# Attention pieces between matmuls: scores, the next pair's q and k, a pause, values in one piece, a pause, probabilities eight at a time

## The chip, the cores and the metric

The kernel runs on one core of a Trainium2 chip. The metric is the device time of one execution in microseconds, as the median of several runs. The kernel before takes 888.13 us (three runs, 887.55 to 888.17).

## What is computed

Three stages follow each other: an attention over 4 batches of 8 heads (576 tokens, 64 elements a head), a feed-forward layer with a gated activation, and a second, bilinear feed-forward layer. The attention is the sum of two: one over means of 4 neighbouring tokens, repeated 4 times, and one over the 7 tokens that lie closer than 4.

```python
q_d = q.reshape(B, H, Sd, factor, D).mean(axis=3)        # the same for k and v; factor = 4
out_up = np.repeat(sm_attn(q_d, k_d, v_d), factor, axis=2)
mask = np.abs(pos[:, None] - pos[None, :]) < factor
scores = np.where(mask, scale * np.matmul(q, k.transpose(0, 1, 3, 2)), -1e9)
attn_out = out_up + np.matmul(softmax(scores), v)

h = x @ w_in;  x = (h * sigmoid(1.702 * h)) @ w_out      # 2304 tokens, 512 -> 2048 -> 512
x = ((x @ w1) * (x @ w2) @ w3) @ w_out2                  # 512 -> 1024 -> 1024 -> 512
```

## The kernel before

Two heads form a pair, so there are 16 pairs, four to a batch. Tokens go through the feed-forward layers in five blocks of 512, 512, 512, 256 and 512. All large products are made of three matmuls of 128 rows (high times low, low times high, high times high; mm3, L118 to L120), with weights that are decoded and split by ACT, DVE and POOL. The weights come from float64 words: DVE decodes them with L173, L176 and L179, which write st and dec. Three staging buffers st and two dec take turns once the first 24 weights are through.

The order of the large work is: the product w34 = w3 times w_out2 (16 steps, each transposed on TensorE from a decoded w3 tile, copied by ACT at L574 and completed by DVE at L575, names w3t and ps_w); then blocks 0 to 4 of the first feed-forward layer (h_step and y_step, names ps_h, ps_y, g_t, gl); then the second layer (ps_ab, ps_o). "Block 0" is always the first token block.

The attention is cut into pieces, and a pump puts one piece after every three matmuls (in the w34 product, which carries batch 0) or after every six (blocks 0 to 2, which carry batches 1 to 3). An entry None in the list is a pause: nothing is put there. A pair goes through four stages:
- T: q and k are transposed into qT and kT, in four pieces (two for q, two for k). In batches 0 and 1 TensorE does it (L284, ps_t) and ACT copies the result (L285); in batches 2 and 3 DVE does it (L280). The means qd and kd are summed on POOL (L294, L296) or on DVE.
- S: three pieces. Two of local scores (L333, ps_s; DVE masks them at L336 into el and takes the maximum at L337) and one of pooled scores (L352, ps_sp). Then the softmax: with own_exp ACT makes one exponential for each of 15 tiles and sums as it goes (L313, after three L311 on DVE); without own_exp DVE subtracts the maximum (L358 for ep, L362 for el), ACT makes two large exponentials (L364, L366) and DVE sums them (L367, L369). L371 and L372 form the reciprocal; POOL (DVE in batch 3) multiplies el and ep with it (L375, L377).
- P: the probabilities are transposed on TensorE (L395, ps_pt) in pieces of up to four tiles and copied by ACT into PT (L396). The first piece also sums the means of v on POOL (v_means).
- V: three pieces. Pooled values (L410, ps_vp, ACT copies od at L413) and two of local values (L422, ps_v; DVE adds od into xo at L426; a DMA writes it to x_d, from where the blocks read it).

The tiles ps_t, ps_s, ps_sp, ps_pt, ps_vp and ps_v all come from one pool of two PSUM buffers, tag t. xo and the results w34s of the w34 product share two buffers, tag ys. The pairs 12 to 15 (batch 3) have no local scores on TensorE; DVE and POOL compute these in small steps beside the blocks.

The stages are lined up in att_pieces: S of a pair, V of the pair before, T of the next pair, P of the pair. The loads of q and k are issued in p_piece and s_pool, two pairs ahead. own_exp is set for batch 0, not for batch 1, and for batches 2 and 3.

The instructions are put in order, engine by engine, when the program is built, by a scheduler that works from the code's order and from priorities; what stands in a queue is therefore shown from the order of the built program.

## Time and profile before

| | us |
|---|---|
| median of 3 runs | 888.13 |
| the profiled execution | 892.31 |
| its span, first to last instruction | 890.5 |
| TensorE (PE) busy | 846.0 (95%) |
| DVE busy | 589.5 (66%) |
| ACT busy | 408.7 (46%) |
| POOL busy | 150.6 (17%) |

A share over the whole span says little here: from about 470 us on TensorE works without a gap, and all of the attention lies before that. The rows below are therefore taken by stretches: 0 to 56 us (first weights, a third of the w34 product), 56 to 120 us (the rest of it, batch 0), 120 to 262 us (block 0, batch 1). Block 1 with batch 2 ends near 381 us. Busy times of matmuls are modelled and overlap; distances from start to start are firmer.

### The profile page before, as it was taken

How to read it: one execution, taken by the hardware profiler on the slowest of the kernel's cores; microseconds unless marked ns; L12 is line 12 of the kernel's file. 1: busy time of each engine (PE TensorE's matmuls, PEld its weight loads, DVE VectorE, ACT ScalarE, POOL GpSimd, SP SyncE). 2: the span in 40 equal slices, each digit the busy share in tenths (PEclk: the TensorE clock that was granted, in tenths of full speed). 3: DMA queues.
4: the chain of work that ended last, by engine and by line, in shares of the span. 5: the costliest groups of instructions: out<-in, count | busy, mean ns of one | idle time of the engine just before them, and what ended most of it. 6: DMA issues, size and time to landing. Idle time of an engine off the chain costs nothing.

```text
span 890.5 us, 13711 instructions
## 1 busy us (share of the span) xinstructions
PE 846.0 (95%) x5132; PEld 712.1 (80%) x5132; DVE 589.5 (66%) x1053; ACT 408.7 (46%) x862; POOL 150.6 (17%) x153
## 2 busy tenths in 40 slices
PE   5789979999999999999999999999999999999998
PEld 4567757666677777777789988889999899989996
DVE  5997587889998795847758973253456455555551
ACT  4667567567657665455446663342112211232111
POOL 7524241244332323311200000000000000000000
PEclk9799999999999999999999999999999999999999
DMA  8865584565656243553348989102556364635521
GB/s 239 270 207 160 155 249 129 163 182 170 158 156 123 63 108 87 131 126 62 78 148 304 358 325 348 49 1 86 210 196 259 105 244 166 255 135 222 191 84 71
DMA packets 140598, 150.76 MB, mean 169 GB/s; under 512 B 86898, under 2 KB 121460, under 8 KB 136436
## 3 DMA queue, kind: packets, MB, share of 16 engines
q1 hardware_dynamic: 119424, 141.21, 49.1%
q10 hardware_dynamic: 21108, 8.69, 4.0%
q8 instruction: 40, 0.66, 0.3%
q14 instruction: 26, 0.21, 0.1%
HBM read 117.75 MB, written 32.11 MB: 168 GB/s over the span
## 4 chain that ended last, share of the span: by engine, by line
PE 72%; DVE 12%; DMA 7%; issue 3%; ACT 3%; POOL 2%; ACTq 0%; SPq 0%; DVEq 0%; POOLq 0%
PE ps_ab L120 7%; PE ps_ab L118 7%; PE ps_ab L119 7%; PE ps_h L118 6%; PE ps_y L118 5%; PE ps_y L120 5%; PE ps_h L119 5%; PE ps_y L119 5%; PE ps_h L120 5%; PE ps_o L120 4%; PE ps_o L119 4%; PE ps_o L118 4%; DMA st<-in_moe_w_in_dram 3%; DVE dec L179 2%; DVE st L176 2%
## 5 line engine op out<-in xcount | busy, mean ns | idle before, releaser
L118 PE MATMUL ps_h<-x_t,w 128*128 128x512 f32 (+1 forms) x320 | 122.7, 385 | 3.0 <-DVE w L115 2.0
L118 PE MATMUL ps_y<-gh,w 128*128 128x512 f32 (+1 forms) x320 | 122.5, 383 | 0.0
L119 PE MATMUL ps_h<-x_t,w 128*128 128x512 f32 (+1 forms) x320 | 119.2, 372 | 1.1 <-DVE x_t L115 1.1
L119 PE MATMUL ps_y<-gl,w 128*128 128x512 f32 (+1 forms) x320 | 118.8, 371 | 0.4 <-DVE gl L115 0.4
L120 PE MATMUL ps_y<-gh,w 128*128 128x512 f32 (+1 forms) x320 | 119.2, 372 | 0.0
L120 PE MATMUL ps_h<-x_t,w 128*128 128x512 f32 (+1 forms) x320 | 118.5, 370 | 0.0
L120 PE MATMUL ps_ab<-b_t,a_in 128*128 128x384 f32 x336 | 112.5, 335 | 0.0
L118 PE MATMUL ps_ab<-b_t,a_in 128*128 128x384 f32 x336 | 112.5, 335 | 0.0
L119 PE MATMUL ps_ab<-b_t,a_in 128*128 128x384 f32 x336 | 112.4, 334 | 0.0
L115 DVE TENSOR_TENSOR gl<-g_t,gh 128x512 fp32r<-128x512 f32 (+1 forms) x80 | 55.0, 690 | 65.8 <-ACT gh L114 65.5
L624 ACT ACTIVATE g_t<-ps_h 128x512 f32<-128x512 f32 (+1 forms) x80 | 44.3, 555 | 92.0 <-PE ps_h L120 87.9
L114 ACT ACTIVATE abh<-ab 128x384 fp32r<-128x384 f32 x24 | 12.7, 527 | 137.5 <-DVE ab L749 137.5
L118 PEld LDWEIGHTS ps_h<-x_t,w 128*128 128x128 f32 x320 | 60.5, 190 | 17.2 <-DVE w L115 3.7
L118 PEld LDWEIGHTS ps_y<-gh,w 128*128 128x128 f32 x320 | 60.5, 189 | 11.8 <-issue 2.4
L119 PEld LDWEIGHTS ps_h<-x_t,w 128*128 128x128 f32 x320 | 60.8, 190 | 11.0 <-DVE x_t L115 2.2
L120 PEld LDWEIGHTS ps_y<-gh,w 128*128 128x128 f32 x320 | 60.5, 189 | 10.4
L120 PEld LDWEIGHTS ps_h<-x_t,w 128*128 128x128 f32 x320 | 60.5, 189 | 10.4 <-issue 0.2
L119 PEld LDWEIGHTS ps_y<-gl,w 128*128 128x128 f32 x320 | 60.6, 189 | 9.3 <-DVE gl L115 0.5
L118 PEld LDWEIGHTS ps_ab<-b_t,a_in 128*128 128x128 f32 x336 | 63.1, 188 | 0.9
L119 PEld LDWEIGHTS ps_ab<-b_t,a_in 128*128 128x128 f32 x336 | 63.1, 188 | 0.9
L179 DVE SCALAR_TENSOR_TENSOR dec<-dec,st 128x512 int32<-128x512 int32 x72 | 59.3, 833 | 6.0 <-ACT dec L166 4.8
L120 PEld LDWEIGHTS ps_ab<-b_t,a_in 128*128 128x128 f32 x336 | 63.1, 188 | 0.0
(150 smaller groups left out, 1667.3 us busy)
## 6 DMA issues: line engine op xcount, KB each, us to landing
a_in<-a_d SPq DMA_DIRECT2D x24, 1792.0 KB
st<-in_moe_w_dram SPq DMA_DIRECT2D x32, 512.0 KB
a_d<-ap SPq DMA_DIRECT2D x8, 1792.0 KB
st<-in_moe_w_out_dram SPq DMA_DIRECT2D x24, 512.0 KB
st<-in_moe_w_in_dram SPq DMA_DIRECT2D x16, 512.0 KB
yr<-y_d SPq DMA_DIRECT2D x12, 384.0 KB
out_dram<-osb SPq DMA_DIRECT2D x17, 256.0 KB
s_v<-in_v_dram ACTq DMA_DIRECT2D x15, 288.0 KB
```

Source lines behind the costliest of these rows:

```text
L114: nc.scalar.activation(hi, raw, AF.Copy)
L115: lo_eng.tensor_tensor(lo, raw, f32(hi), op=ALU.subtract)
L118: nc.tensor.matmul(ps, ll, rh, start=start, stop=False, skip_group_check=more)
L119: nc.tensor.matmul(ps, lh, rl, start=False, stop=False, skip_group_check=more)
L120: nc.tensor.matmul(ps, lh, rh, start=False, stop=stop, skip_group_check=more)
L176: nc.vector.scalar_tensor_tensor(low, st[:, :, 1], -0x80000000, low, op0=ALU.bitwise_and, op1=ALU.bitwise_or)
L179: nc.vector.scalar_tensor_tensor(t, t, 3, st[:, :, 0], op0=ALU.logical_shift_left, op1=ALU.bitwise_or)
L624: nc.scalar.activation(g[:, :n], ps[:, :n], AF.Gelu_apprx_sigmoid)
```

## The change

- The order in att_pieces becomes: S of a pair, T of the next pair, two pauses, V of the pair before, three pauses (two in batch 0), P of the pair.
- T has two pieces instead of four: both halves of q at once, then both halves of k. Each is followed by the load of the next pair's q or k, which leaves p_piece and s_pool.
- V is one piece, v_all: pooled and local values go into two PSUM buffers without a break, the pooled ones and the second local half in one buffer; then od, then the two xo, second half first. For the pairs of batch 3, v_far does the pooled values as before.
- P is done up to eight tiles at a time, with a pause between.
- Batch 0 no longer uses own_exp.

```diff
@@ t_piece, s_pool, p_piece: the loads of q and k
+            if 0 < n < B * HP - 1:
+                att_load(n + 1, name)
...
-        if n % HP == 0 and n > 0:
-            att_load(n + 1, "qk")
...
-            if n % HP < HP - 1 and n + 2 < B * HP:
-                att_load(n + 2, "qk")
@@ values
+    def v_all(n):
+
+        both = pst.tile([128, NB], F32, tag="t", name="ps_v")
+        rest = pst.tile([128, NB], F32, tag="t", name="ps_v")
+        local = ((HQ, NQB, both[:, SD:SD + (NQB - HQ) * QB]), (0, HQ, rest[:, :HQ * QB]))
+        v_pool_mm(n, both[:, :SD])
+        for i0, i1, ps in local:
+            v_local_mm(n, i0, i1, ps)
+        v_pool(n, both[:, :SD])
+        for i0, i1, ps in local:
+            v_local(n, i0, i1, ps)
+        if n + 1 < B * HP and n + 1 not in LOCAL:
+            att_load_v(n + 1)
@@ stage
+        def together(*fns):
+            return [None] * (len(fns) - 1) + [lambda: [fn() for fn in fns]]
+
         if what == "T":
-            return [lambda name=name, c=c: t_piece(n, name, c) for name in "qk" for c in range(2)]
+            return [together(*(
+                lambda name=name, c=c: t_piece(n, name, c) for c in range(2)))[-1] for name in "qk"]
...
         if what == "P":
-            return [lambda i=i: p_piece(n, i, min(i + 4, NPT)) for i in range(0, NPT, 4)]
-        return [lambda: v_pool(n), lambda: v_local(n, 0, HQ), lambda: v_local(n, HQ, NQB)]
+            return [p for i in range(0, NPT, NPH) for p in together(*(
+                lambda i=i: p_piece(n, i, min(i + 4, NPT)) for i in range(i, min(i + NPH, NPT), 4)))][1:]
+        return [lambda: v_all(n)]
@@ att_pieces
             out_ += stage(n0 + i, "S", own_exp)
+            if i + 1 < HP:
+                out_ += stage(n0 + i + 1, "T", own_exp)
+            out_ += [None] * 2
             if i > 0:
                 out_ += stage(n0 + i - 1, "V", own_exp)
-            if i + 1 < HP:
-                out_ += stage(n0 + i + 1, "T", own_exp)
-            else:
-                out_ += [None] * rest
+            out_ += [None] * (2 if b == 0 else 3)
             out_ += stage(n0 + i, "P", own_exp)
@@ batch 0
-        pump = Pump(att_pieces(0, True, 3))
+        pump = Pump(att_pieces(0, False, 3))
```

Three places show what this does to the order. The first is TensorE at the start of block 0, where pair 4, the first of batch 1, begins: s_k is its k, ps_t the transpose, ps_s and ps_sp its local and pooled scores. Before:

```order
L120 MATMUL ps_h<-x_t,w 128x512
L284 MATMUL ps_t<-ident,s_k 128x72 x4
L118 MATMUL ps_h<-x_t,w 128x512
L119 MATMUL ps_h<-x_t,w 128x512
L120 MATMUL ps_h<-x_t,w 128x512
L284 MATMUL ps_t<-ident,s_k 128x72 x4
L333 MATMUL ps_s<-kT,qT 64x72 x18
L352 MATMUL ps_sp<-kd,qd 64x144 x6
L118 MATMUL ps_h<-x_t,w 128x512 x2
```

After, from the second local piece on (the transposes of s_k stand 24 full matmuls ahead of it):

```order
L335 MATMUL ps_s<-kT,qT 64x72 x8
L118 MATMUL ps_y<-gh,w 128x512
L119 MATMUL ps_y<-gl,w 128x512
L120 MATMUL ps_y<-gh,w 128x512
L118 MATMUL ps_y<-gh,w 128x512
L119 MATMUL ps_y<-gl,w 128x512
L120 MATMUL ps_y<-gh,w 128x512
L352 MATMUL ps_sp<-kd,qd 64x144 x6
```

The pooled scores, which need the sums qd and kd, stood directly behind the transposes and the local scores, and now 30 full matmuls behind the transposes.

The second place is DVE in the softmax of the same pair 4, from the subtraction L362 to the reciprocal L372 (st, dec, w and gl are weights and activations of the block). Before, in its first part:

```order
L354 TENSOR_REDUCE mx<-ps_sp 128x3
L362 TENSOR_TENSOR el<-el,mx 128x648
L358 TENSOR_TENSOR ep<-ps_sp,mx 128x432
L179 SCALAR_TENSOR_TENSOR dec<-dec,st 128x512
L173 TENSOR_SCALAR st<-st 128x512
L115 TENSOR_TENSOR gl<-g_t,gh 128x512
L173 TENSOR_SCALAR st<-st 128x512
L176 SCALAR_TENSOR_TENSOR st<-st 128x512 x2
L179 SCALAR_TENSOR_TENSOR dec<-dec,st 128x512
L115 TENSOR_TENSOR gl<-g_t,gh 128x512
L173 TENSOR_SCALAR st<-st 128x512
L115 TENSOR_TENSOR w<-dec,w 128x512
```

After:

```order
L362 TENSOR_TENSOR el<-el,mx 128x648
L179 SCALAR_TENSOR_TENSOR dec<-dec,st 128x512
L115 TENSOR_TENSOR gl<-g_t,gh 128x512
L354 TENSOR_REDUCE mx<-ps_sp 128x3
L358 TENSOR_TENSOR ep<-ps_sp,mx 128x432
L369 TENSOR_REDUCE sm<-el 128x9
L115 TENSOR_TENSOR gl<-g_t,gh 128x512
L367 TENSOR_REDUCE sm<-ep 128x3
L173 TENSOR_SCALAR st<-st 128x512
L371 TENSOR_SCALAR sm<-sm 128x12
L176 SCALAR_TENSOR_TENSOR st<-st 128x512
L372 RECIPROCAL sm<-sm 128x12
```

Before, the sums L367 and L369 stood behind all of the rows shown and seven more of weights; now the whole softmax takes twelve rows with one L173, which may wait for a load.

The third place is DVE late in the w34 product, between the eleventh w3t (step 10) and the twelfth. After:

```order
L372 RECIPROCAL sm<-sm 128x12
L176 SCALAR_TENSOR_TENSOR st<-st 128x512
L115 TENSOR_TENSOR x_t<-xr,x_t 128x512
L179 SCALAR_TENSOR_TENSOR dec<-dec,st 128x512
L173 TENSOR_SCALAR st<-st 128x512
L176 SCALAR_TENSOR_TENSOR st<-st 128x512
L173 TENSOR_SCALAR st<-st 128x512
L176 SCALAR_TENSOR_TENSOR st<-st 128x512
L173 TENSOR_SCALAR st<-st 128x512
L446 TENSOR_TENSOR xo<-ps_v,od 128x256
L601 TENSOR_TENSOR w3t<-ps_w,w3t 128x512
```

The last L173 here is that of the 28th weight; before, only 24 had been begun when the twelfth w3t came, and now the xo of pair 1 and the twelfth w3t stand behind the 28th.

## Rows read from the trace of the kernel before

**Rows 1.** Windows: stretch, its length, busy us (count) by engine, clock, DMA share, GB/s.
```profile
0.00:56.00 56.00, 34.63 (x213) 26.79 (x215) 43.70 (x67) 30.32 (x68) 32.02 (x49) 0.89 0.78 241
56.00:120.00 64.00, 60.91 (x541) 46.68 (x538) 48.26 (x90) 43.17 (x131) 24.43 (x26) 0.97 0.62 178
120.00:262.00 142.00, 128.44 (x883) 97.38 (x882) 123.38 (x201) 89.03 (x148) 46.45 (x43) 0.98 0.59 166
```

**Rows 2.** Waits of PE, 0 to 56 us: us in total, times, longest.
```profile
PE ps_w L573 <- DVE dec L179: 16.4, 4, 9.0
PE ps_w L118 <- DVE w3t L575: 4.0, 2, 3.5
```

**Rows 3.** Waits of PE, 120 to 262 us.
```profile
PE ps_sp L352 <- POOL kd L296: 3.7, 1, 3.7
PE ps_pt L395 <- ACT kT L285: 2.5, 2, 1.7
PE ps_pt L395 <- POOL el L375: 2.1, 1, 2.1
PE ps_h L118 <- DVE w L115: 2.0, 3, 0.8
PE ps_pt L395 <- ACT PT L396: 1.3, 1, 1.3
```

**Rows 4.** Timeline of POOL, pair 4.
```profile
151.90 1.27 POOL L375 TENSOR_TENSOR el<-el,sm 128x648 f32<-128x648 f32 x1 [19.94 <-DVE sm L372]
```

**Rows 5.** Timeline of PE around two runs of local values.
```profile
107.47 0.39 PE L120 MATMUL ps_w<-w,w3t 128*128 128x512 f32 x1
107.70 0.39 PE L118 MATMUL ps_w<-w,w3t 128*128 128x512 f32 x1
108.02 0.80 PE L422 MATMUL ps_v<-PT,vw 72*64 72x64 f32 x20
...
109.09 0.39 PE L120 MATMUL ps_w<-w,w3t 128*128 128x512 f32 x1
...
331.56 0.39 PE L118 MATMUL ps_y<-gh,w 128*128 128x512 f32 x1
331.88 1.27 PE L422 MATMUL ps_v<-PT,vw 72*64 72x64 f32 x36
...
333.42 0.39 PE L120 MATMUL ps_y<-gh,w 128*128 128x512 f32 x1
```

**Rows 6.** Timeline of PE around four transposes of probabilities.
```profile
337.52 0.39 PE L120 MATMUL ps_h<-x_t,w 128*128 128x512 f32 x1
337.75 0.60 PE L395 MATMUL ps_pt<-ident,el 128*72 128x128 f32 x4
...
338.42 0.40 PE L119 MATMUL ps_y<-gl,w 128*128 128x512 f32 x1
```

**Rows 7.** Groups of DVE by line and form: busy us, mean ns, idle before.
```profile
L369 DVE TENSOR_REDUCE sm<-el 128x9 f32<-128x648 f32 x4 | 3.3, 823 | 0.0
L362 DVE TENSOR_TENSOR el<-el,mx 128x648 f32<-128x648 f32 x4 | 3.3, 822 | 0.0
L358 DVE TENSOR_TENSOR ep<-ps_sp,mx 128x432 f32<-128x432 f32 x4 | 2.4, 598 | 0.0
L367 DVE TENSOR_REDUCE sm<-ep 128x3 f32<-128x432 f32 x4 | 2.4, 596 | 2.1 <-ACT ep L364 2.1
L311 DVE TENSOR_SCALAR nb<-mx 128x3 f32<-128x3 f32 x12 | 1.9, 160 | 0.1
```

**Rows 8.** Timeline of DVE and of POOL, 42 to 46 us.
```profile
42.52 1.77 DVE L179 SCALAR_TENSOR_TENSOR dec<-dec,st 128x512 int32<-128x512 int32 x1
45.14 0.68 DVE L179 SCALAR_TENSOR_TENSOR dec<-dec,st 128x512 int32<-128x512 int32 x1
42.22 1.52 POOL L115 TENSOR_TENSOR w<-dec,w 128x512 fp32r<-128x512 f32 x1
```

**Rows 9.** Chain that ended last, a load of a weight.
```profile
102.83 4.40 DMA st<-in_moe_w_in_dram
```

More of the change, by code (lines that the diff above doesn't have):

```diff
@@ L399, in p_piece, with v_far, v_pool_mm @@
             v_means(n)
-            if n % HP < HP - 1 and n + 2 < B * HP:
-                att_load(n + 2, "qk")
-    def v_pool(n):
+    def v_all(n):
[10 more added lines that the diff above has]
+            att_load_v(n + 1)
+    def v_far(n):
+        ps = pst.tile([128, SD], F32, tag="t", name="ps_vp")
+        v_pool_mm(n, ps)
+        v_pool(n, ps)
+    def v_pool_mm(n, ps):
         PT, vd = at["PT", n, 1], at["vd", n]
-        ps = pst.tile([128, SD], F32, tag="t", name="ps_vp")
         for kc in range(2):
@@ L411, in v_pool, with v_local_mm @@
                     ps[p], vd[:, h, kc], PT[:, i:i + NPB, h * QB:h * QB + PB], start=kc == 0, stop=kc == 1)
+    def v_pool(n, ps):
         at["od", n] = od = att.tile([128, SD], F32, tag="od", name="od")
         nc.scalar.activation(od, ps, AF.Copy, scale=1.0 / FAC)
-    def v_local(n, i0, i1):
-        vw, od = at["vw", n, i0 // HQ], at["od", n]
-        xo = g2p.tile([128, NB], F32, tag="ys", name="xo")[:, :(i1 - i0) * QB]
-        ps = pst.tile([128, (i1 - i0) * QB], F32, tag="t", name="ps_v")
+    def v_local_mm(n, i0, i1, ps):
+        vw = at["vw", n, i0 // HQ]
         for i in range(i0, i1):
@@ L424, in v_local @@
                     start=True, stop=True)
+    def v_local(n, i0, i1, ps):
+        od = at["od", n]
+        xo = g2p.tile([128, NB], F32, tag="ys", name="xo")[:, :(i1 - i0) * QB]
         u0, u1 = i0 * UB, i1 * UB
@@ L430, in v_local @@
         nc.sync.dma_start(out=x_d[:, hp, b * S + i0 * QB:b * S + i1 * QB], in_=xo)
-        if i1 == NQB and n + 1 < B * HP and n + 1 not in LOCAL:
-            att_load_v(n + 1)
     def l_load(n):
@@ L518, in stage @@
             if what == "P":
-                return [lambda: p_piece(n, NPH, NPH + 4), lambda: p_piece(n, NPH + 4, NPT)]
-            return [lambda: v_pool(n), lambda: l_out(n, 0, HQ), lambda: l_out(n, HQ, NQB)]
+                return together(lambda: p_piece(n, NPH, NPH + 4), lambda: p_piece(n, NPH + 4, NPT))
+            return [lambda: v_far(n), lambda: l_out(n, 0, HQ), lambda: l_out(n, HQ, NQB)]
         if what == "S":
```

## The prediction

> **What bounds the kernel now.** I read first the windows, one row per stage of the first half [rows 1]. The reader is to see two engines in them. TensorE is busy 34.6 of the first 56 us, then 60.9 of 64 and 128.4 of 142; behind them it has hardly a gap. So what can be won is what TensorE loses before 262 us, 21.4 + 3.1 + 13.6 us, and the price of its own small instructions. DVE is the other: 43.7 of 56, 48.3 of 64, 123.4 of 142.
>
> Then the list of waits, TensorE's alone, stage by stage. Up to 56 us it waits for DVE: 16.4 us for decoded weights (9.0 of it the first load) and 4.0 us for the low half of a transposed w3 tile [rows 2]. From 120 to 262 us (token block 0, with batch 1 of the attention in it) the longest are 3.7 us for the pooled k, 2.5 us in which a transpose waits for ACT's copy kT, 2.1 us for the probabilities, 2.0 us for a split weight, 1.3 us for ACT's copy PT [rows 3].
>
> Last the timeline of POOL in that stage: before it multiplied the probabilities of pair 4, the first of batch 1, it sat idle for 19.94 us and waited for DVE's reciprocal [rows 4]. The cause is the place of the softmax sums in DVE's order: between the subtraction and the sums stand the decodes and splits of several weights.
>
> **The change part by part.** The sum is made against the profiled execution, 892.31 us (span 890.5 and 1.8 around it), and then carried to the median, 888.13, as a difference.
>
> *Fewer switches.* Two plain neighbours start 0.23 us apart. Twenty matmuls of 64 rows between them stretch two such distances from 0.46 to 109.09 - 107.70 = 1.39 us, a cost of 0.93; thirty-six cost 333.42 - 331.56 - 0.46 = 1.40. The slope is 0.47 / 16 = 0.029 us a matmul, and 0.93 - 20 x 0.029 = 0.35 remains for going in and out [rows 5]. v_all makes one run of up to three. Counted in the order, the runs of half-height matmuls go from 69 to 58: 19 to 15 before block 0, 20 to 16 in block 0, 22 to 19 in block 1, 8 and 8 in block 2. In blocks 0 and 1, where TensorE is full, that is 7 x 0.35 = -2.4 us. The four in the first stage (-1.4) I count within it. Transposes four or eight at a time change nothing: four of them cost 338.42 - 337.52 - 0.46 = 0.44, or 0.11 each with nothing left over [rows 6]. The q and k transposes are as many as before.
>
> *Batch 0 without its own exponentials.* Each of four pairs gains on DVE L362, L358, L369 and L367, 0.82 + 0.60 + 0.82 + 0.60 = 2.84 us, and loses three L311 of 0.16: +2.36 us [rows 7]. ACT has fifteen exponentials a pair less and two long ones more, but TensorE waits for DVE there and not for ACT [rows 2], so that gives nothing. The bounds: at least 0 (DVE's 56 - 43.7 = 12.3 idle us swallow it; no gain, since DVE only gets more to do), at most 4 x 2.36 = +9.4. Up to 56 us TensorE stands behind DVE, and the softmax of pairs 0 and 1 falls into this stretch and just behind it; there nothing hides it. Later DVE waits for weights (64 - 48.3 = 15.7 us idle) and can hide pairs 2 and 3. I take 2 x 2.36 = +4.7, with the four switches +3.3.
>
> *The start of block 0.* Before, the last k transposes, the scores and the pooled scores of pair 4 stand in TensorE's order with nothing between; afterwards 30 full matmuls lie between k and the first pooled score, 30 x 0.23 = 6.9 us and the local scores. That covers the 3.7 us. Also the last values of batch 0 come 20 full matmuls earlier than before, so their xo have left the two ys buffers when ACT wants to write w34s there, ahead of the copies of q and k. Of the two ends, 0 and -3.7, I take -3.7 whole.
>
> *Probabilities.* For a pair with a predecessor the pooled scores stood 8 slots before the first P piece, now 9, for the first pair of a batch 5 and now 8; transposes of the next pair no longer stand directly in front of P, where P waited for their copies (2.5 us). What can go is 2.5 + 2.1 + 1.3 = 5.9 us. At most all of it goes; at least nothing, if only the next thing becomes late. That next thing is there: DVE has 142 - 123.4 = 18.6 us idle in this stage, part of it waits for weights, and TensorE already waits 2.0 us for a split weight. I take a third, -2.0: the time gained on probabilities is given back for weights, mostly.
>
> *Waits that are new.* T stands directly behind S, and both use the two PSUM buffers of tag t: the second q transpose needs the buffer of the pooled scores, which DVE frees with L358. Queued behind it on TensorE are all matmuls of the block. The order leaves 6 to 20 full matmuls there, 1.4 to 4.6 us; L354 and L358 take 0.6 each: no cost, and if DVE is held up by a weight, what that wait lasts. v_all needs both buffers at once and gives them back only after od and two xo; the first P piece stands 3 slots later, which in blocks 0 and 1 is 18 full matmuls, 4.1 us: nothing. The loads of q and k go out on ACT one by one behind the copies; they have a whole pair's time. In block 2 the pieces end 60 full matmuls later than before, but 66 are left before block 3 needs x, 66 x 0.23 = 15.2 us: nothing.
>
> The sum: -2.4 + 3.3 - 3.7 - 2.0 = -4.8, so 887.5 for this execution and 888.13 - 4.8 = 883.3 for the median.
>
> One rule of the Trainium skill speaks against the second part. While POOL ran L115 a decode of DVE took 1.77 us, alone 0.68, a loss of 1.1 [rows 8]. "SBUF — State Buffer", section "Who interferes with whom", says that a DVE instruction with two SBUF inputs and a GpSimd one that reads SBUF hold a shared port exclusively, one blocking the other to its end; the trace agrees. L362 has two such inputs, and now the sums of the next pair's q and k on POOL run during it. By the rule it is a rival, priced below.
>
> **The rivals.**
> *The first stage pays for all (slower).* DVE's order puts four decodes of the next weights before the twelfth w3t. The staging buffers are three: the transfer of the fourth starts when the first of the four is decoded, and takes 4.40 us [rows 9]. All DVE work behind it stands still, xo of pair 1 too, and so the PSUM buffers that P needs. With no cover for the four softmaxes: +9.4 + 4.4 - 1.4 (switches) - 2.4 - 3.7 = +6.3, 894.4. It decides at step 11 of the w34 product, if TensorE stands there longer than 2 us. For it: DVE's 43.7 of 56. Against: DVE idles 15.7 us in the next 64.
> *Nothing is gained in block 0 (no change).* The pace there is transfer, decode, split; TensorE waits for weights for as long as it waited for attention: +3.3 - 2.4 = +0.9, 889.0. For it: DVE's 123.4 of 142. Against: part of DVE's idle time is itself the wait for pooled scores.
> *All of it works.* Waits -3.7 - 5.9, switches 11 x 0.35 = -3.9, the first stage free: -13.5, 874.6. For it: the order of DVE puts the softmax of pair 4 together; against, the same 43.7 of 56.
> *The port.* Four times 1.1 us on top of the forecast: 887.7. For it the same row; against, that in the first stage decodes lose the same time to POOL already.
>
> **How the numbers follow.** Forecast 0.42, the slower rival 0.20, no change 0.18, all of it 0.14, the port 0.06. About 0.2%, 1.8 us, can be told from no change, so faster is below 886.4 and slower above 889.9. The forecast's own range is 878 to 888: 0.37 faster, 0.05 same. The slower rival: 0.17 slower, 0.03 same. No change: 0.04, 0.10, 0.04. All of it: faster. The port: 0.02 and 0.04. Together 0.57, 0.22, 0.21. The range of 8 in 10 reaches from the end of "all of it" to the slower rival, 874 to 894.5.
>
> **What would show it.** Right: in the profile after, no wait of ps_sp for kd at the start of block 0; ps_v runs of 44 records (each of the 4 pooled and 18 local matmuls leaves two) that cost about 0.35 us less than apart; the w34 product ending 2 to 5 us later than 120 us; TensorE's waits for split weights in block 0 longer than 2.0. Wrong: a stand of over 4 us at w34 step 11 (the slower rival); w waits of 6 us or more in block 0 (no change); the first stage no longer than before (all of it); L362 of 1.5 us and more (the port). A wait at the start of block 3 would show that the later end of batch 3 matters after all.

## The result and the profile after

The changed kernel takes 897.74 us (median of four runs, 895.37 to 898.93) against 888.15 before; the ratio is 1.0105, with a 95% interval of 1.008 to 1.013. It is 9.6 us slower. I had predicted 883.3, and 894.5 as the upper end: the change goes the other way, and the time lies above the range. The profiled execution took 898.85 us, span 897.0. Of the kernel before there is a second profile by now, span 884.4 (e5 below), so a stage of one profile is only good to a few us; I compare with the mean of both. Three of the 67 later runs of the kernel before, and one of e9, were in a slower state of the chip (943.94 us and more) and are in no ratio and no mean below.

To place the loss I number the full matmuls, those of mm3 in the large products (L118 to L120), from 0 in TensorE's order, and read from the traces when the n-th starts: the 192nd opens token block 0, the 576th block 1, the 1344th block 3, the 2112th the second layer. From there all kernels take 273.9 us to the 3551st, the last. The last line of the table is a clock for the weights: when DVE ends its 50th L179, the last step of a decode.

```
                            before (two profiles)   after
block 0 begins                 120.1   117.2        131.1
block 0 lasts                  140.9   138.6        136.1
blocks 1 and 2 last            217.1   216.3        215.1
blocks 3 and 4 last            134.4   134.3        136.7
50th decode of a weight ends   216.9   215.0        223.1
```

Against the mean of before that is +12.5 in the first stage, -3.7, -1.6 and +2.3: +9.5 in all. The windows that answer to [rows 1]:

```profile
0.00:56.00 56.00, 32.52 (x204) 24.76 (x204) 43.71 (x64) 27.50 (x46) 36.99 (x49) 0.85 0.84 245
56.00:120.00 64.00, 54.23 (x455) 41.87 (x456) 57.69 (x92) 29.83 (x55) 24.97 (x25) 0.92 0.61 173
120.00:262.00 142.00, 133.15 (x953) 102.77 (x951) 118.41 (x196) 93.85 (x157) 40.58 (x44) 0.98 0.56 160
```

DVE, the third busy time of a row, went from 48.26 to 57.69 us in the 64 us from 56 to 120, and ACT from 43.17 to 29.83. TensorE lost 6.7 us of busy time there, and its granted clock is 0.92 in place of 0.97. What TensorE waits for in the first stage, up to 56 us (this answers to [rows 2]), and then from 56 to 131:

```profile
PE ps_w L599 <- DVE dec L179: 11.7, 3, 8.9
PE ps_w L599 <- DVE w3t L601: 3.4, 1, 3.4
PE ps_w L118 <- DVE w3t L601: 2.0, 1, 2.0
```

```profile
PE ps_pt L395 <- DVE xo L446: 6.9, 2, 4.4
PE ps_w L599 <- DVE w3t L601: 3.4, 1, 3.4
PE ps_pt L395 <- POOL el L375: 1.9, 1, 1.9
```

The new wait is the first row of the second list: the probabilities wait for a PSUM buffer that DVE gives back with xo. A stand is a time in which TensorE waits. TensorE at the longer of the two stands for xo:

```profile
94.50 0.50 PE L118 MATMUL ps_w<-w,w3t 128*128 128x512 f32 x1
...
95.99 0.39 PE L118 MATMUL ps_w<-w,w3t 128*128 128x512 f32 x1
100.81 0.70 PE L395 MATMUL ps_pt<-ident,el 128*72 128x128 f32 x4 [4.42 <-DVE xo L446]
```

Seven full matmuls run between the values, which end at 94.5, and the stand. (xo is made in two halves; the one shown frees the buffer that TensorE takes next.) DVE in that time:

```profile
92.25 1.76 DVE L115 TENSOR_TENSOR x_t<-xr,x_t 128x512 fp32r<-128x512 f32 x1
93.93 1.39 DVE L179 SCALAR_TENSOR_TENSOR dec<-dec,st 128x512 int32<-128x512 int32 x1
95.25 0.67 DVE L173 TENSOR_SCALAR st<-st 128x512 int32<-128x512 int32 x1
95.95 0.94 DVE L176 SCALAR_TENSOR_TENSOR st<-st 128x512 int32<-128x512 int32 x1
96.93 0.67 DVE L173 TENSOR_SCALAR st<-st 128x512 int32<-128x512 int32 x1
97.63 1.09 DVE L176 SCALAR_TENSOR_TENSOR st<-st 128x512 int32<-128x512 int32 x1
99.90 0.43 DVE L173 TENSOR_SCALAR st<-st 128x512 int32<-128x512 int32 x1 [1.18 <-DMA st<-in_moe_w_out_dram]
100.24 0.42 DVE L446 TENSOR_TENSOR xo<-ps_v,od 128x256 f32<-128x256 f32 x1
```

The two buffers are full from 94.5 on, and xo stands behind six instructions on weights, the last of which waits for a load. This is the third place shown under the change, and the mechanism of my slower rival. Right behind the stand, from 101.2 to 104.6 us, the granted clock is half: full matmuls start 0.42 us apart in place of 0.23.

From 131 to 270 us, block 0, the answer to [rows 3]:

```profile
PE ps_h L118 <- DVE w L115: 3.4, 2, 2.6
PE ps_sp L352 <- DVE el L338: 2.3, 1, 2.3
...
PE ps_pt L395 <- POOL el L375: 1.1, 2, 0.7
```

No wait for kd, kT or PT is left, but split weights (3.4 us, before 2.0) cost more than before, and the pooled scores now wait 2.3 us for a buffer that DVE gives back with the masking of local scores (L338). POOL's row for pair 4 [rows 4] now has no idle time directly in front of it, and comes 22.4 us behind the begin of block 0 where it came 31.8:

```profile
153.51 1.72 POOL L375 TENSOR_TENSOR el<-el,sm 128x648 f32<-128x648 f32 x1
```

The values in one run, the answer to [rows 5], here in block 1:

```profile
373.72 0.39 PE L120 MATMUL ps_y<-gh,w 128*128 128x512 f32 x1
374.04 0.71 PE L426 MATMUL ps_v<-PT,vd 72*64 72x144 f32 x8
374.58 1.22 PE L438 MATMUL ps_v<-PT,vw 72*64 72x64 f32 x36
375.73 0.50 PE L118 MATMUL ps_y<-gh,w 128*128 128x512 f32 x1
376.06 0.39 PE L119 MATMUL ps_y<-gl,w 128*128 128x512 f32 x1
```

It costs 376.06 - 373.72 - 0.46 = 1.88 us. The three runs of before (8, 16 and 20 matmuls) cost, by medians of the same distance, 0.85 + 0.82 + 0.94 = 2.61: the two switches saved are 0.36 each, as predicted.

### The profile page after: what moved, and what is told of

It is laid out like the page before. It is cut to its first block, busy times and chain, and to the rows that moved or that the text cites. A ratio compares the mean times of both kernels' runs of the same rounds, so it can differ in the third digit from the quotient of the medians.

```text
span 897.0 us, 13629 instructions
## 1 busy us (share of the span) xinstructions
PE 846.0 (94%) x5132; PEld 715.8 (80%) x5132; DVE 599.7 (67%) x1057; ACT 398.4 (44%) x778; POOL 151.8 (17%) x153
## 4 chain that ended last, share of the span: by engine, by line
PE 65%; DVE 18%; DMA 7%; ACT 4%; issue 4%; POOL 1%; ACTq 0%; SPq 0%; DVEq 0%; POOLq 0%
PE ps_ab L120 7%; PE ps_ab L118 7%; PE ps_ab L119 7%; PE ps_h L118 5%; PE ps_h L119 5%; PE ps_h L120 5%; PE ps_y L120 5%; PE ps_y L119 5%; PE ps_y L118 4%; PE ps_o L119 4%; PE ps_o L120 4%; PE ps_o L118 4%; DVE dec L179 3%; DVE st L176 3%; DMA st<-in_moe_w_in_dram 3%
## 5 line engine op out<-in xcount | busy, mean ns | idle before, releaser
L118 PE MATMUL ps_h<-x_t,w 128*128 128x512 f32 (+1 forms) x320 | 121.7, 382 | 5.9 <-DVE w L115 3.4
L118 PE MATMUL ps_y<-gh,w 128*128 128x512 f32 (+1 forms) x320 | 120.0, 377 | 0.0
L120 PE MATMUL ps_y<-gh,w 128*128 128x512 f32 (+1 forms) x320 | 119.3, 373 | 0.0
L120 PE MATMUL ps_h<-x_t,w 128*128 128x512 f32 (+1 forms) x320 | 118.6, 371 | 0.0
L120 PE MATMUL ps_ab<-b_t,a_in 128*128 128x384 f32 x336 | 112.5, 335 | 0.0
L118 PE MATMUL ps_ab<-b_t,a_in 128*128 128x384 f32 x336 | 112.5, 335 | 0.0
L115 DVE TENSOR_TENSOR gl<-g_t,gh 128x512 fp32r<-128x512 f32 (+1 forms) x80 | 53.3, 668 | 61.1 <-ACT gh L114 60.8
L118 PEld LDWEIGHTS ps_h<-x_t,w 128*128 128x128 f32 x320 | 60.5, 190 | 20.2 <-DVE w L115 4.6
L114 ACT ACTIVATE abh<-ab 128x384 fp32r<-128x384 f32 x24 | 12.6, 526 | 137.5 <-DVE ab L775 137.5
L118 PEld LDWEIGHTS ps_y<-gh,w 128*128 128x128 f32 x320 | 60.5, 189 | 10.6 <-issue 0.6
L120 PEld LDWEIGHTS ps_h<-x_t,w 128*128 128x128 f32 x320 | 60.6, 189 | 10.3
L120 PEld LDWEIGHTS ps_y<-gh,w 128*128 128x128 f32 x320 | 60.6, 189 | 10.3 <-issue 0.4
L179 DVE SCALAR_TENSOR_TENSOR dec<-dec,st 128x512 int32<-128x512 int32 x72 | 61.2, 861 | 4.8 <-ACT dec L166 4.3
L118 PEld LDWEIGHTS ps_ab<-b_t,a_in 128*128 128x128 f32 x336 | 63.1, 188 | 0.9
L120 PEld LDWEIGHTS ps_ab<-b_t,a_in 128*128 128x128 f32 x336 | 63.1, 188 | 0.0
```

Source lines behind the costliest of these rows:

```text
L114: nc.scalar.activation(hi, raw, AF.Copy)
L115: lo_eng.tensor_tensor(lo, raw, f32(hi), op=ALU.subtract)
L118: nc.tensor.matmul(ps, ll, rh, start=start, stop=False, skip_group_check=more)
L120: nc.tensor.matmul(ps, lh, rh, start=False, stop=stop, skip_group_check=more)
L179: nc.vector.scalar_tensor_tensor(t, t, 3, st[:, :, 0], op0=ALU.logical_shift_left, op1=ALU.bitwise_or)
```

## The experiments

Eighteen kernels were run, one of them (e5) the kernel before again; the before of each comparison ran on the same chip, with medians of 887.5 to 890.3. The ratio is that to this before, with its 95% interval. The columns behind it come from one profile each: when block 0 begins, how long block 0, blocks 1 and 2, and blocks 3 and 4 last, when the 50th decode ends.

```
      median  ratio [95%]               begins  0      1,2    3,4    50th
e1    896.68  1.0070 [1.0044, 1.0096]   120.1  144.6  216.8  135.4  222.4
e2    896.15  1.0068 [1.0042, 1.0095]   133.3  129.8  217.5  135.7  221.4
e3    897.54  1.0087 [1.0056, 1.0118]   124.0  136.3  218.2  137.0  217.4
e4    899.74  1.0100 [1.0070, 1.0130]   132.8  132.8  220.9  134.3  222.7
e6    893.86  1.0053 [1.0029, 1.0078]   126.9  135.1  217.1  135.8  220.4
e7    897.71  1.0106 [1.0061, 1.0151]   116.9  140.8  221.6  135.3  214.5
e8    899.61  1.0120 [1.0073, 1.0167]   128.0  140.5  219.5  135.3  223.0
e9    890.21  0.9991 [0.9960, 1.0022]   121.7  137.8  215.5  134.3  218.5
e10   905.18  1.0163 [1.0130, 1.0196]   123.0  142.6  225.1  134.3  221.9
e11   892.37  1.0032 [1.0012, 1.0052]   117.8  139.9  218.1  134.3  216.9
e12   902.75  1.0152 [1.0101, 1.0202]   128.3  141.0  218.5  135.8  227.6
e13   898.32  1.0109 [1.0073, 1.0145]   130.4  137.9  216.7  134.3  229.5
e14   900.21  1.0128 [1.0092, 1.0165]   131.8  135.6  219.0  133.8  225.3
e15   904.20  1.0190 [1.0138, 1.0241]   132.0  135.7  222.0  134.7  225.1
e16   906.30  1.0202 [1.0159, 1.0245]   126.7  146.2  217.8  134.3  231.8
e17   899.33  1.0099 [1.0068, 1.0129]   134.5  135.6  215.0  136.1  226.0
e18   900.06  1.0111 [1.0060, 1.0162]   121.9  142.4  216.7  135.4  222.0
```

### Halves of the change (e1, e2)

e1 is the changed kernel with the old batch 0:

```
+        if n < HP:
+            if what == "T":
+                return [lambda name=name, c=c: t_piece(n, name, c) for name in "qk" for c in range(2)]
...
+        if b == 0:
+            for i in range(HP):
...
-        pump = Pump(att_pieces(0, False, 3))
+        pump = Pump(att_pieces(0, True, 3))
```

> The first stage (batch 0, beside the making of w34) keeps the old pieces, order, loads and its own exponentials; batches 1 to 3 have the new pieces. No engine's order differs from the kernel before until block 0 of the tokens begins, so TensorE must start its 192nd full matmul near 120.1 us, as before. Theory A (the first stage alone loses, and what the traces give the token blocks 0 and 1, 4.8 and 2.7 us, is the change's own gain): the end is 888.15 - 7.5 and some 2 us back that the later blocks lost between the two traces: 881 to 884. Theory B (the token blocks only made up for a late start: weights were decoded ahead while they waited): nothing is to be made up here, and the time is 887 to 890.

Both theories fell. Block 0 began at 120.1 as it had to, and then took 144.6 us, longer than before. Three rows show where it began to lose: DVE in e1, then SP, which issues the loads of weights, in the kernel before, and the load of the same weight in e1.

```profile
129.82 0.53 DVE L338 TENSOR_TENSOR el<-ps_s,band 128x360 f32<-128x360 f32 x1 [5.24 <-POOL kd L294]
```

```profile
130.26 0.57 SPq L149 DMA_DIRECT2D st<-in_moe_w_out_dram  x1
```

```profile
142.46 0.33 SPq L149 DMA_DIRECT2D st<-in_moe_w_out_dram  x1
```

The scores of pair 4 had moved ahead of a decode in DVE's order; DVE stood 5.24 us, the staging buffer came free late, the load went out 12 us later, and TensorE then waited 7.6 us for split weights. So the 3.7 us less of block 0 in the changed kernel can't be put down to the attention's pieces.

e2 is the opposite half, with the same stage function for batches 1 to 3 in place of batch 0. The loads of q and k stay where the change has put them, in all batches.

```
+        if n >= HP and (n not in LOCAL or what == "T"):
+            if what == "T":
+                return [lambda name=name, c=c: t_piece(n, name, c) for name in "qk" for c in range(2)]
...
+        if b > 0:
+            for i in range(HP):
```

> The opposite half: batch 0 has the new pieces, order and loads without its own exponentials, batches 1 to 3 the old pieces. Orders equal the changed kernel's until block 0 begins, so the 192nd full matmul must start near 131 us, 11 later than before. Theory A: all of it is kept to the end: 897 to 900. Theory B: the old blocks make up 5 to 7 us of it as well: 891 to 894.

896.15 lies between the two forecasts, 0.9 below the one and 2.2 above the other, but the profile is clear on the point: the old block 0, begun 14.6 us late, took 129.8, some 10 us less than when it begins on time. A late first stage is made up for in large part; the weights go on being decoded while TensorE is late (32 decodes are begun before block 0 in place of 29).

### The exponentials of batch 0 (e3, e4)

```
-        pump = Pump(att_pieces(0, False, 3))
+        pump = Pump(att_pieces(0, True, 3))
```

> The changed kernel, but batch 0 keeps its own exponentials (per block with the row sums from ScalarE), so VectorE is free again of the subtractions and sums: 4 pairs of 2.36 us. Theory S (these sums are what the first stage pays): most of 9.4 us comes back in the first stage, the 192nd full matmul starts at 122 to 124 instead of 131.1 and the time is 889 to 892. Theory V (the values in one piece hold both transpose buffers until VectorE comes to their last sum, and the probabilities wait for them): the stands at the probabilities stay, the 192nd full matmul is at 128 or later, and the time is 895 to 898.

```
-        pump = Pump(att_pieces(0, True, 3))
+        pump = Pump(att_pieces(0, False, 3))
```

> The kernel before, with only this: batch 0 without its own exponentials, so VectorE does the subtractions and sums, 4 pairs of 2.36 us. Theory S: the 192nd full matmul comes 5 to 10 us after the 120.1 of before, and the time is 892 to 897. Theory V: VectorE has room for them while no transpose buffer is held for it, and the time is 887 to 890.

Alone, giving the exponentials up (e4) took the time from 890.21 to 899.74. That this is about the 9.4 us of DVE's work, my upper bound, is luck: it is made of +14.1 in the first stage, -7.0 in block 0 and +4.2 in blocks 1 and 2. The longest waits of TensorE in the first 60 us, where before they were [rows 2]:

```profile
PE ps_w L573 <- DVE dec L179: 11.3, 2, 9.0
PE ps_w L573 <- DVE w3t L575: 8.7, 1, 8.7
```

Taking them back in the changed kernel (e3) gave 7.1 us in the first stage and nothing that can be told at the end.

### Variation, the other mixture, and spaced transposes (e5 to e8)

e5 is the kernel before, unchanged.

> The kernel before, unchanged, for a second profiled execution, to see how far the stages of one kernel vary: if each stage's end (192nd full matmul, end of token blocks 0 and 1) lies within 1 us of the first profile (120.1, 261.0, 379.2), the differences of 3 us and more read between the kernels are of the kernels; if they move by 3 us, single profiles can't carry them.

It took 886.18 us; blocks 0, 1 and 2 begin 2.9, 5.2 and 5.9 us earlier than in the first profile. A single profile can't carry a difference of 3 us.

e6 is e2 with `Pump(att_pieces(0, True, 3))`.

> Batch 0 in the new pieces, order and loads but with its own exponentials; batches 1 to 3 old. Seen so far against before: own exponentials away in the old order +9.5 (e4), new batch 0 without them +5.9 (e2). Theory add (the parts add up; the new order of batch 0 is worth 5.9 - 9.5 = -3.6 by itself): 884 to 887. Theory stream (not TensorE's place but the stream of weight decodes on VectorE sets the end of token block 0; the new order of batch 0 moves TensorE and leaves the decodes): no change, 888 to 891.

893.86: the parts don't add up (this was to be 884 to 887), and it is no "no change" either. Block 0 begins 8 us late and is 4.6 us shorter.

```
-                out_ += stage(n0, "T", own_exp) + [None] * rest
+                out_ += [p for t in stage(n0, "T", own_exp) for p in (t, None)] + [None] * rest
```

> The kernel of e1 (batch 0 old, token blocks new) with one edit: in the token blocks the first pair of a batch has a pause behind each of the two transposing pieces, so that they stand as far apart as the four pieces of before. In VectorE's order two weight decodes then stand ahead of the first scores of block 0; in e1 they stood behind, VectorE waited 5.2 us for the scores' transposes, and the next weight load was issued at 142.5 us instead of 130.3. Theory stream: the stand goes, the 40th decode ends near 171 instead of 176, and most of the 6.5 us of e1 come back: 886 to 891. Theory values (the values in one piece and the probabilities by eight cost in every block): 894 to 897.

e7 has this edit on e1. The local part came true: the 40th decode ended at 166.1 in place of e1's 176.0. The time did not: what block 0 won in its first half (69.0 us, e1 80.0) it gave back in its second (71.9, e1 64.6) and in blocks 1 and 2 (221.6, e1 216.8). e8 has both edits on the changed kernel:

> The changed kernel with its own exponentials in batch 0 and, in the token blocks, the pauses of e7: both suspected causes undone, the rest of the change kept. Theory stream: 885 to 890, the same as before or faster. Theory values: 894 to 898, as e3.

899.61, with a block 0 of 140.5. Theory stream, as I had put it, with one place in DVE's order as the cause, fell.

### One part alone on the kernel before (e9 to e12)

```
-            return [lambda name=name, c=c: t_piece(n, name, c) for name in "qk" for c in range(2)]
+            return [t for name in "qk" for t in together(*(
+                lambda name=name, c=c: t_piece(n, name, c) for c in range(2)))]
```

> The kernel before, with only the transposes of q (and of k) in one piece of eight in place of two of four; the piece stands where the second of the two stood, so no later piece moves. Theory one part (one of the edits carries the 6.5 us that the new token blocks cost in e1, and the values in one piece are the likeliest): 886 to 890 here. Theory any order (each edit moves weight decodes and loads behind pieces that wait, whichever it is): 892 to 896 here as well.

```
-            return [lambda i=i: p_piece(n, i, min(i + 4, NPT)) for i in range(0, NPT, 4)]
+            return [p for i in range(0, NPT, NPH) for p in together(*(
+                lambda i=i: p_piece(n, i, min(i + 4, NPT)) for i in range(i, min(i + NPH, NPT), 4)))]
...
```

> The kernel before, with only the probabilities transposed eight at a time (both fours in the slot of the second). Theory one part: 885 to 889, by the switches and waits saved on TensorE (my prediction had 2.0 us for it). Theory any order: 892 to 896.

```
-        return [lambda: v_pool(n), lambda: v_local(n, 0, HQ), lambda: v_local(n, HQ, NQB)]
+        return [lambda: v_all(n), None, None]
...
```

> The kernel before, with only the products with the values in one piece (both transpose buffers taken at once, given back after the last sum on VectorE), in the slot of the first of the three old pieces, then two pauses. Theory one part: 893 to 898, and waits of the next transposes for the sums of VectorE stand in the first stage. Theory any order: 892 to 896 as well, but then e9, e10 and e12 are as slow.

```
+            if 0 < n < B * HP - 1:
+                att_load(n + 1, name)
...
-            if n % HP < HP - 1 and n + 2 < B * HP:
-                att_load(n + 2, "qk")
```

> The kernel before, with only the loads of the next pair's q and k moved to the end of the transposing pieces. Theory one part: 887 to 891. Theory any order: 892 to 896.

Neither theory got it. The transposes alone cost nothing and the values, which I had under suspicion, only 2.8 us; the probabilities cost 14.5 and the mere move of the loads 13.5 (ratios times the median of before). In e10 TensorE and DVE around 200 us:

```profile
199.79 0.72 PE L333 MATMUL ps_s<-kT,qT 64*64 64x72 f32 x16
204.06 0.79 PE L119 MATMUL ps_y<-gl,w 128*128 128x512 f32 x1 [3.55 <-DVE gl L115]
```

```profile
199.82 0.43 DVE L173 TENSOR_SCALAR st<-st 128x512 int32<-128x512 int32 x1 [2.10 <-DMA st<-in_moe_w_out_dram]
200.28 0.70 DVE L176 SCALAR_TENSOR_TENSOR st<-st 128x512 int32<-128x512 int32 x1
202.25 0.43 DVE L173 TENSOR_SCALAR st<-st 128x512 int32<-128x512 int32 x1 [1.27 <-DMA st<-in_moe_w_in_dram]
202.72 0.69 DVE L176 SCALAR_TENSOR_TENSOR st<-st 128x512 int32<-128x512 int32 x1
203.33 0.68 DVE L115 TENSOR_TENSOR gl<-g_t,gh 128x512 fp32r<-128x512 f32 x1
```

And in e12 DVE and TensorE around 91 us:

```profile
90.30 0.43 DVE L173 TENSOR_SCALAR st<-st 128x512 int32<-128x512 int32 x1 [2.73 <-DMA st<-in_moe_w_out_dram]
...
91.69 0.49 DVE L424 TENSOR_TENSOR xo<-ps_v,od 128x320 f32<-128x320 f32 x1 [0.24 <-DMA vw<-in_v_dram]
```

```profile
92.23 0.47 PE L284 MATMUL ps_t<-ident,s_q 72*128 72x72 f32 x4 [2.68 <-DVE xo L424]
```

In these two stands it's the figure of the changed kernel again: a small instruction of DVE that TensorE needs (gl, xo) stands behind the first step L173 of a decode, and that waits for its load. The two are not the whole loss: in e12 TensorE also stood 4.1 us for probabilities (POOL's el), 3.6 us for a buffer of scores and 4.7 us for gl up to 270 us.

### One part undone in the changed kernel (e13 to e16)

e13 undoes the loads (the diff of e12 backwards), e14 the probabilities:

```
-            return [p for i in range(0, NPT, NPH) for p in together(*(
-                lambda i=i: p_piece(n, i, min(i + 4, NPT)) for i in range(i, min(i + NPH, NPT), 4)))][1:]
+            return [lambda i=i: p_piece(n, i, min(i + 4, NPT)) for i in range(0, NPT, 4)]
...
-            out_ += [None] * (2 if b == 0 else 3)
+            out_ += [None] * (1 if b == 0 else 2)
```

> The changed kernel with one part undone: the loads of the next pair's q and k stand again where they stood (first probabilities piece, first scores of a batch). Theory loads (alone on the kernel before they cost 13.5 us in e12; what the change pays is mostly this part): 886 to 892. Theory own and order (the loads matter only in the old order; here the sums of batch 0 and the held buffers pay): 895 to 900.

> The changed kernel with the probabilities again in fours, the first four one slot earlier, one pause fewer. Theory probabilities (alone they cost 14.5 us in e10, by stands of TensorE long enough that its clock falls): 886 to 892. Theory own and order: 895 to 900.

e15 has the values in three pieces again, e16 is e13 with `Pump(att_pieces(0, True, 3))`:

```
-        return [lambda: v_all(n)]
+        return [lambda: v_far(n), lambda: v_near(n, 0, HQ), lambda: v_near(n, HQ, NQB)]
...
-            out_ += [None] * (2 if b == 0 else 3)
+            out_ += [None] * (0 if b == 0 else 1)
```

> The changed kernel with the values again in three pieces, each with a transpose buffer of its own, two pauses fewer so that nothing behind moves. Theory values (the failed sentence of my prediction; the 6.9 us of waits for the sums at the probabilities of the first stage): these waits go, the 192nd full matmul comes at 125 us or before, and the time is 889 to 893. Theory any other part: 895 to 900, alone it cost 2.8 us in e11.

> The changed kernel with old loads and with its own exponentials in batch 0. Theory loads: 884 to 889, at or ahead of the kernel before; theory order (the order of the pieces itself, scores, transposes, values, probabilities, pays in the first stage): 893 to 897, as e3 with 897.5.

None gave the time back; e15 and e16 made it worse. In e15, with a buffer for each piece in turn, the wait for xo is as long as in the changed kernel (8.1 us against 6.9), so that v_all takes both at once is not what holds the probabilities:

```profile
PE ps_pt L395 <- DVE xo L453: 8.1, 2, 4.4
```

In e13 the wait for xo is nearly gone (1.2 us), and from the 36th to the 192nd full matmul TensorE takes 77.9 us, as before; but block 0 still begins at 130.4, because TensorE had stood 10.8 us for the first probabilities:

```profile
33.27 8.51 POOL L300 TENSOR_TENSOR s_v<-s_v 72x512 f32<-72x512 f32 x1 [3.01 <-DMA s_v<-in_v_dram]
50.04 1.92 PE L395 MATMUL ps_pt<-ident,el 128*72 128x128 f32 x8 [10.78 <-POOL el L375]
```

The same sum on POOL (L300) took 1.26 us in the kernel before. DVE has its extra work in e13 as well, and the time of one wait stands in another. e13 shows one thing more: with the old loads blocks 3 and 4 take 134.3 us again. Over all profiles, those with old loads (both of before, e4, e9, e10, e11, e13, e16) have 134.3 or 134.4; of those with moved loads two have 133.8 and 134.7, the other ten 135.3 to 137.0. The changed kernel's 136.7 is 2.3 us of its loss. Of these, 1.8 us are waits of TensorE around the start of block 4 (2.2 us, for x_t and gl above all, against 0.4 in e13); what makes x late there I have not traced.

### The buffers freed by another engine (e17, e18)

```
+        if n < HP:
+            nc.scalar.activation(xo, ps, AF.Copy)
+            ps = xo
         nc.vector.tensor_tensor(
```

> The changed kernel with one edit: in batch 0 ScalarE copies the products with the values out of their transpose buffers right behind the pooled part, and VectorE adds the pooled part to the copy later. Nothing else moves by more than a few rows; the buffers no longer wait for VectorE, and VectorE's work is the same. Theory buffers (the probabilities of the first stage wait for sums that stand behind weight decodes on VectorE, and the clock falls after such stands): the 6.9 us of waits for the sums go, the stretch from the 36th to the 192nd full matmul falls from 90.1 us to 80 to 84, and the time is 888 to 892. Theory VectorE (the first stage is as long as VectorE's work, and a wait that goes is put elsewhere): the waits go over to decodes, the stretch stays at 87 to 90, and the time is 895 to 898.

> As e17, and batch 0 keeps its own exponentials, so that the transpose buffers are freed by ScalarE and VectorE loses its 9.4 us of subtractions and sums as well. Theory VectorE: the stretch from the 36th to the 192nd full matmul falls to 76 to 79 (75.9 and 78.9 before), and the time is 888 to 892. Theory buffers: 886 to 890, at or ahead of before. Theory order (as e3, 897.5): 895 to 898.

In e17 the waits for xo are gone, and the same time stands at the w3t tiles, which DVE makes too (9.5 us where the changed kernel has 3.4), and at POOL's el; 56 to 135 us:

```profile
PE ps_w L602 <- DVE w3t L604: 9.5, 3, 3.4
PE ps_pt L395 <- POOL el L375: 3.8, 1, 3.8
```

The stretch from the 36th to the 192nd full matmul took 93.2 us and the time is 899.33, even above what theory VectorE allowed. (By the estimate further down 13.2 of the 93.2 us are lost to the clock, 7.9 of the changed kernel's 90.0; without that the freed buffers would be worth 2.2 us. The stretch alone does not decide it, the waits that went over do.) In e18, with DVE's extra work gone, the stretch fell to 79.5, nearly before's.

That is the fifth pair of kernels that differ in the exponentials of batch 0 alone. Without them block 0 begins later each time: by 14.1 us (the mean of before to e4), 7.1 (e3 to the changed kernel), 6.4 (e6 to e2), 3.7 (e16 to e13) and 12.6 (e18 to e17); e3 and e8, whose first stage is written the same, differ by 4.0, so the pair with 3.7 says nothing alone. So the softmax that DVE took over is what makes the first stage long. Whether by its time on DVE alone or also because the way from scores to probabilities has more steps (DVE, ACT, DVE again, POOL) is not separated.

Yet e18 takes 900.06: block 0 begins at 121.9 and lasts 142.4, its clock is 0.94, and DVE waits 17.6 us for weight loads there. From 122 to 264 us, TensorE's longest wait and DVE's two:

```profile
PE ps_h L118 <- DVE w L115: 5.0, 2, 4.7
```

```profile
DVE st L173 <- DMA st<-in_moe_w_out_dram: 10.8, 5, 3.5
DVE st L173 <- DMA st<-in_moe_w_in_dram: 6.8, 6, 3.2
```

## Why the prediction was wrong

**The step that failed** is the term of the sum for the first stage: "I take 2 x 2.36 = +4.7, with the four switches +3.3". Found are +12.5. Of the 14.3 us between the sum (-4.8) and the stages (+9.5) 9.2 are here; 3.4 are block 0 (-1.4 for switches, -3.7 and -2.0, found -3.7), 2.3 are blocks 3 and 4, for which I had nothing, and blocks 1 and 2 give 0.6 back. I took two of the four pairs as paid and hid the other two in DVE's 15.7 idle us; and for the lower bound I read 12.3 idle us up to 56, of which 7.1 lie in the first 12 us, ahead of any softmax. About half of the 15.7 us is DVE waiting for weight loads (7.7 us; in the second profile 7.7 of 13.0 us from 41 to 117). The rows of L173 from 41 us to the start of block 0, of the kernel before (e5) and after:

```profile
L173 DVE TENSOR_SCALAR st<-st 128x512 int32<-128x512 int32 x19 | 12.6, 671 | 7.7 <-DMA st<-in_moe_w_out_dram 5.1 <-DMA st<-in_moe_w_in_dram 2.6
```

```profile
L173 DVE TENSOR_SCALAR st<-st 128x512 int32<-128x512 int32 x21 | 14.8, 715 | 1.2 <-DMA st<-in_moe_w_out_dram 1.2
```

DVE did take the work into those gaps: from 41 us to the start of block 0 it is busy 83.7 us where it was busy 63.0, and idle 6.3 where it was 13.0. But what TensorE needs from it came later. e13, e15 and e17 show that it is not one wait, e18 that the length goes with DVE's softmax. The waits for loads did not vanish either: in block 0 DVE waits 16.3 us for them (131 to 267 us), before 9.2 (120 to 262).

**A second step failed with it,** in the part on new waits: "the first P piece stands 3 slots later, which in blocks 0 and 1 is 18 full matmuls, 4.1 us: nothing". I worked it out for the token blocks and let it stand for batch 0, where a piece comes after every three matmuls: seven full matmuls, 1.6 us, with xo behind six weight instructions. TensorE waited 6.9 us there. By itself that step does not explain the loss, for with these waits gone (e17) or nearly gone (e13) block 0 begins no earlier than 130 us.

**The clock was missing from the sum.** TensorE's granted clock has two levels here, 2.4 and 1.2 GHz. In the changed kernel the four stands of 2.5, 4.4, 2.6 and 2.3 us that end at 77.6, 100.8, 165.1 and 206.9 us are each followed by a stretch at the lower one. From 41 us on to the 96th full matmul, before (e5) and after (the figure behind the five busy times is the clock):

```profile
41.00:77.00 36.00, 31.46 (x262) 23.86 (x262) 35.25 (x58) 21.27 (x57) 16.30 (x16) 0.92 0.69 195
```

```profile
41.00:83.00 42.00, 33.82 (x259) 26.11 (x259) 41.14 (x60) 18.27 (x35) 21.85 (x19) 0.85 0.60 168
```

An estimate of what that costs, with TensorE taken as busy throughout: the share of the clock not granted times the span, as a mean over the runs, is 12.0 us in 64 runs of before and 15.9 in the four of after. So up to 3.9 of the 7.6 us between the mean spans (888.0 and 895.6) are clock. In the profiles it lies in the first stage: up to block 0 13.7 us after against 8.5 and 6.8 before, in block 0 3.4 in all three. In e10 the figure of the runs is 22.1, which is 10.1 of its 15.1.

**The gains in block 0.** Switches: 0.36 us each, right. The kd wait is gone, right; that block 0 as a whole is shorter by the same 3.7 us is chance. Probabilities: kT and PT waits gone, el down to 1.1, so more went than the third I took. And weights take their place, as I said (w 2.0 to 3.4, plus 2.3 for the pooled scores' buffer, which my sum did not have). But the balance I read as a gain isn't one: with the same new pieces and the old first stage (e1) block 0 lasts 144.6 us, with the old pieces after a late start (e2) 129.8. Its end goes with the weights. Over the twenty profiles the end of the 50th decode and the end of block 0 correlate at 0.94, the begin of block 0 and its end at 0.73. That is a correlation, not a proof; e18 fits it, where the begin of block 0 came back to within 3.2 us and the end, with the weights, did not. That weights set the end of block 0 is argued and not shown.

**The rivals.** "The first stage pays for all" had mechanism and place right: TensorE stood 4.4 us, more than its 2, and its 894.4 is nearer than my forecast. Its +12.4 for the first stage (9.4 + 4.4 - 1.4) meets the 12.5 found in part by luck, since it has no clock in it, which by the estimate is up to 6.0 of them, and since more than one wait makes them up; what it lacks is for the most part blocks 3 and 4. I gave it 0.20 and kept 883.3 because DVE had idle time behind the start; that reason was the error. "All of it works" fell with the first stage, which was to be no longer than before. "No change" named weights as what rules block 0, which fits but is not shown. The port: L362 takes 0.856 us in the mean (1.08 at most) where it took 0.822 [rows 7], so there is little of it there, though L179 and L176 of the first stage are longer than in e5 (1.026 and 0.881 us against 0.958 and 0.807, 22 of each, 3 us in all) while POOL is busier (39.7 us from 41 us to block 0, in e5 29.4). That agrees with what the Trainium skill ("SBUF — State Buffer", "Who interferes with whom") says of POOL and DVE, that one can block the other at a port they share, and stands in other instructions than I had priced. It is largest on POOL: while DVE decodes without a gap, one split of POOL takes 5.95 us in the changed kernel (1.39 for L115 at 31.87 us of before):

```profile
34.47 5.95 POOL L115 TENSOR_TENSOR w<-dec,w 128x512 fp32r<-128x512 f32 x1 [4.32 <-ACT w L114]
```

A POOL instruction of 5 us or more in the first 56 us stands in all seven profiles in which batch 0 lacks its own exponentials (among them e13's 8.51 us, with TensorE's stand of 10.8 us behind it) and in none of the other thirteen. What it costs in the changed kernel no run separates.

**"They have a whole pair's time"**, said of the loads of q and k and priced at nothing, is the third wrong step: alone 13.5 us (e12), in the changed kernel the 2.3 us of blocks 3 and 4, which went when they were put back (e13); the whole time did not come back with them.

**What stays open.** Which part of the change costs what: by the ratios, alone they cost 8.9 (exponentials), 13.5 (loads), 14.5 (probabilities), 2.8 (values) and nothing (transposes), together 9.3, and no single one undone gives anything back at the end. In the changed kernel, e10 and e12 I can show a stand behind a decode that waits; why the weight loads come late just there I can't, nor did I run the order of the pieces (transposes ahead of values) by itself. Of the eighteen altered kernels, the changed one among them, only e9 is level with before and only e11 else is within 0.5% of it; none is faster.

## What to carry to other kernels

Don't count an engine's idle time as cover before you have seen what it waits for. Here half of it was a wait for loads: work put there pushed back what stood behind it, and the other engine that waited for a small result paid. Where a stream of loads and decodes runs through a stage, ask of each moved piece what it puts ahead of the next decode, and what small instruction is caught behind a decode that waits; count slots at the rate of the stage they are in. And test an edit by itself before adding its gain to others': here the parts did not add up.

## What was not expected of the hardware

A stand of TensorE cost more than itself: after the one of 4.42 us that ended at 100.81 the granted clock was half from 101.2 to 104.6 us, and after those of 2.3 to 2.6 us it fell as well. An instruction of POOL took 5.95 and 8.51 us, in place of some 1.3, while DVE worked through decodes without a gap. In e10 the stretch from 192 to 237 us ran at a granted clock of 0.89. And executions of one kernel differ in their stages by up to 5.9 us between two profiles (span 890.5 and 884.4), so that a single profile shows where a kernel stands, not by how much it is slower.
